# Feed-forward part ordered by a graph of needed-by times, with more seven-product chunks

## Chip, cores and metric

The kernel runs on one core of a Trainium2 chip. The metric is device time in microseconds (us); the median of the runs counts. Engines: PE (TensorE) multiplies matrices and writes PSUM; ACT (ScalarE) and DVE (VectorE) read and write PSUM and SBUF; POOL (GpSimd) works on SBUF alone; SP (SyncE) issues most DMA transfers. Each engine takes its instructions in order.

## Reference

One token block of 2048 rows and width 576 goes through a linear-attention block and through a feed-forward block, and a per-row gate mixes the two.

```python
def _B_ref(x, w1, b1, w2, b2):
    y = _layernorm(x, axis=-1)
    h = _gelu(jnp.einsum("bsd,df->bsf", y, w1) + b1)      # w1: 576 x 4608
    return jnp.einsum("bsf,fd->bsd", h, w2) + b2          # w2: 4608 x 576
x = A_x
g = _sigmoid((x * gate_w).sum(-1, keepdims=True))
a = _A_ref(x, A_wqkv, A_wo)       # linear attention, 32 heads of 18
b = _B_ref(x, B_w1, B_b1, B_w2, B_b2)
return g * a + (1 - g) * b
```

The inputs are float32. Every factor is split into a rounded high part and a low part, so a product is made of high x high, high x low and low x high.

## Kernel before

The attention part comes first (up to about 279 us) and is the same in both kernels, but for the stores named below. Its results, scaled by g, are `acc[0..15]`, sixteen tiles of 128 rows.

The feed-forward part handles the 2048 rows in two halves of 1024 (`NSUP = 2`, `TPS = 8` tiles), and the 4608 hidden columns in 18 chunks of 256 (`NCHUNK`). So there are 36 steps k; `HALF_TIME = 18` begins the second half.

**Up-projection.** Each step computes h for one chunk and 1024 rows as a 2 x 2 block product with seven products in place of eight (Strassen's scheme in Winograd's form, `FACTORS`). One product is seven matmuls of 128 x 512 (`FIVE`), so a step has 49. `A11 ... S4` are the blocks and sums of w1, `B11 ... T4` those of y. Products accumulate in three of four PSUM banks (X, Yb, Z); `kept` copies an intermediate from PSUM to SBUF by ACT, `plus` adds another one by DVE, `gelu` writes the high part and the whole value by ACT and its returned function the low part by DVE.

**Down-projection.** A plain chunk (`down`) makes 8 tiles x 12 matmuls of 128 x 288 = 96, in two alternating PSUM pairs (`ff_pairs`, banks 6-7 and 4-5), and DVE adds each tile, weighted by 1 - g, onto `acc`. A seven-product chunk (`unit`) makes 14 units of 6 matmuls = 84. It needs four sums of w2 blocks (`sum_w2`, POOL, 4 operations) and four sums of h (`sum_h`, POOL, 4 operations), each split by ACT and DVE.

In the first half all 18 chunks are plain. In the second half chunks of steps 18 to 33 (16 of them) are seven-product; each of the seven products has a running sum over all these chunks in `sums` (DVE adds 14 evictions per chunk, ACT writes some of the first), and step 35 puts the seven sums together (`add_sums`, `add_combined`). Steps 34 and 35 (`PLAIN`, `LAST`) are plain.

**Order.** Both loops are written out by hand: the down-projection of step k - 1 runs between the up products of step k, and the jobs for other engines (`later`, `todo`) stand at numbered places. In the first half w1 of the next chunk is loaded, summed (`sum_w1`, POOL), split and stored to DRAM (`w1d`); y of the second half is normalized, summed, split and stored (`load_pair` to `store_pair`). In the second half the split w1 comes back from DRAM, 7 x 320 KB per step, and y is loaded anew at the change of halves. `attend_out` stores the attention tiles of the second half only, to `late_acc`. All instructions pass through one helper, so the profile gives line 109 (`InOrder`) for all; groups are told apart by tile names: `h`, `u` (whole values), `region` (split w2, and other split data), `fresh` (raw w1 and w2), `accs` (sums and accumulators), `wa`, `wb` (split w1), `ps` (PSUM).

Of the kernel before, what the change touches and what calls it, by code (L numbers as in the profile page):

```python
# [43 lines left out]

# [8 lines left out]

FIVE = [(0, 0), (1, 1), (2, 2), (0, 3), (1, 4), (3, 0), (4, 1)]
A11, A12, S2, S1, A21, A22, S3, S4 = range(8)  # L70
FIRST_W, LAST_W = (A11, S1), (A22, S4)
B11, B21, T1, B22, T2, T3, T4 = range(7)

# [4 lines left out]
PLAIN = 2 * NCHUNK - 2  # L78
LAST = 2 * NCHUNK - 1
DOWN_ORDER = (1, 4, 2, 5, 7, 6, 3)  # L80
W2_PLACES = [FACTORS[n][1] for n in DOWN_ORDER]
W2_GROUPS = ((0, 2), (2, 4), (4, 6), (6, 7))
# [30 lines left out]
def tile_gated_mix(ctx: ExitStack, tc: tile.TileContext, x, xm, xe, wm, we, wvm, wve, wo, um, ue, w2, b1, b2, gw, out):  # L113
# [6 lines left out]

# [32 lines left out]
    for _ in range(WARM):  # L153
# [11 lines left out]
    sums = {n: accs[:, i * TPB * HALF:(i + 1) * TPB * HALF].rearrange("p (s n) -> p s n", n=HALF)  # L165
            for i, n in enumerate(DOWN_ORDER)}
# [8 lines left out]
    mrt = keep.tile([2 * max(q1 - q0 for q0, q1 in MOMENTS), P], F32, name="mrt")  # L175
    moments = [dram.tile([2, (q1 - q0) * P], F32, name=f"moments{b}") for b, (q0, q1) in enumerate(MOMENTS)]
    w1d = [dram.tile([P, 7, 5, P], F32, name=f"w1d{c}") for c in range(NCHUNK)]
    late_acc = dram.tile([TPS, P, D], F32, name="late_acc")

# [15 lines left out]

# [119 lines left out]


# [65 lines left out]
    def store_moments(b, p):  # L382
        n = mr[b].shape[1] * mr[b].shape[2]
        act.activation(mrt[:n], p[:n], AF.Copy)
        sp.dma_start(moments[b].rearrange("a (t n) -> (a t) n", n=P), mrt[:n])
# [4 lines left out]

# [30 lines left out]
    def split_pair(sup, j, part, stage):  # L421
        m0, m1 = 2 * part, min(2 * part + 2, 7)
# [316 lines left out]
    for m in (B11, B21, T2, T1, T3, T4, B22):  # L739
        load_y(0, m)  # L740
# [15 lines left out]
    hs, c2s, w2raw = {}, {}, {}  # L756

    def wr(k):
        at_ = fresh[:, :24 * P] if k > 1 else spare[:, :24 * P]
        return at_.rearrange("p (m s n) -> p m s n", m=8, s=3)  # L760
# [9 lines left out]
    def sum_w1(k):  # L770
        r = wr(k)
        for to, x0, x1, op in ((S1, A21, A22, OP.add), (S2, S1, A11, OP.subtract), (S4, A12, S2, OP.subtract),
                               (S3, A11, A21, OP.subtract)):
            pool.tensor_tensor(out=r[:, to], in0=r[:, x0], in1=r[:, x1], op=op)

    def split_w1(k, first):

        a, b = FIRST_W if first else LAST_W
        b += 1
        w = wa if first else wb  # L780
        src = wr(k)[:, a:b]
        act.activation(w[:, :, 0:3], src, AF.Copy)
        dve.tensor_sub(w[:, :, 3:5], src[:, :, 0:2], raw(w[:, :, 0:2]))
        dve.tensor_sub(w[64:P, :, 2], src[64:P, :, 2], raw(w[64:P, :, 2]))
# [4 lines left out]

    def w1_of(a):  # L790
        return wa[:, a] if a <= FIRST_W[1] else wb[:, a - LAST_W[0]]

    def load_split_w1(k, a):
        place = a if a <= FIRST_W[1] else a - LAST_W[0] + 4
        sp.dma_start(raw(w1_of(a)).rearrange("p s n -> p (s n)"),
                     w1d[k % NCHUNK][:, place].rearrange("p s n -> p (s n)"))

    def w2_rows(k):
        c = k % NCHUNK
        return w2[c * CF * P:(c + 1) * CF * P].rearrange("(f p) d -> p f d", p=P)  # L800

    def load_w2(k, to):
        w2raw[k] = to.rearrange("p (f n) -> p f n", f=CF)
        sp.dma_start(w2raw[k], w2_rows(k))

    def split_w2(k, to, parts=(0, 1)):
        c2 = c2s[k] = to.rearrange("p (a f n) -> p a f n", a=2, f=CF)
        if 0 in parts:
            act.activation(c2[:, 0], w2raw[k], AF.Copy)
        if 1 in parts:  # L810
            dve.tensor_sub(c2[:, 1], w2raw[k], raw(c2[:, 0]))

    def product(k, n, p, start=True, part=range(len(FIVE))):
# [5 lines left out]
        if len(FIVE) - 1 in part:  # L819
            if k == HALF_TIME - 1:  # L820
                load_y(1, b)
            if HALF_TIME - 1 <= k < LAST:
                load_split_w1(k + 1, a)
# [7 lines left out]
    def plus(t, p):  # L831
        dve.tensor_tensor(out=t, in0=p, in1=t, op=OP.add)
        return t

    def gelu(k, f, t, src, whole, h=None, split=True):

        bias = b1s[:, k % NCHUNK * CF + f:k % NCHUNK * CF + f + 1]
        if split:
            h = hs[k, f, t] = take_h((k, f, t)) if h is None else h
            act.activation(h[:, 0], src, AF.Gelu_apprx_tanh, bias=bias)  # L840
        act.activation(whole, src, AF.Gelu_apprx_tanh, bias=bias)
        return lambda: dve.tensor_sub(h[:, 1], whole, raw(h[:, 0]))

    TERMS = ((0, 0), (0, 1), (1, 0))
    terms = [(f, a, w) for f in range(CF) for a, w in TERMS]

    def add(i, to, term):
        dve.scalar_tensor_tensor(to, term, omg[:, PLACE[i]:PLACE[i] + 1], to, op0=OP.mult, op1=OP.add)

    def down_terms(p, s, k, half, only=range(len(terms)), opens=True, closes=True):  # L850
        c0 = s % TPB * P
        for n in only:
            f, a, w = terms[n]
            pe.matmul(p, hs[k, f, s // TPB][:, a, c0:c0 + P], c2s[k][:, w, f, half_cols(half)],
                      start=opens and n == 0, stop=closes and n == len(terms) - 1)

    def down(k, s):

        if k >= 0:
            p = two_of(ff_pairs)[:, :, :HALF]  # L860
            for n in range(len(terms)):
                for half in range(2):
                    down_terms(p[:, half], s, k, half, (n,))
            if s % TPB == TPB - 1:
                give_back_h((k, 0, s // TPB), (k, 1, s // TPB))
            add(s, halves(acc[s]), p)
            if k == 1 + s:
                add(s, acc[s], b2b)
            if k == HALF_TIME - 1:
                sp.dma_start(out[s * P:(s + 1) * P, :], acc[s])  # L870
        for job in later.get((k + 1, s), ()):
            job()
# [3 lines left out]
    b2b = ffc.tile([P, D], F32, name="b2b")  # L876
    wa = ffc.tile([P, FIRST_W[1] - FIRST_W[0] + 1, 5, P], F32R, name="wa")
    wb = ffc.tile([P, LAST_W[1] - LAST_W[0] + 1, 5, P], F32R, name="wb")

# [4 lines left out]
    extra[3] += [lambda: sp.dma_start(b2b, everywhere(b2, D))]  # L884
    extra[5] += [lambda: sum_w1(0), lambda: act.activation(tiny, ones[:, 0:1], AF.Gelu_apprx_tanh)]
    extra[7] += [lambda: split_w1(0, True), lambda: store_w1(0, True)]
    extra[9] += [lambda: split_w1(0, False), lambda: load_w1(1), lambda: store_w1(0, False)]
    extra[11] += [lambda: sum_w1(1)]

# [17 lines left out]

    h_places = ctx.enter_context(tc.tile_pool(name="hp", bufs=1)).tile([P, 6, 2, SB], F32R, name="h")
    h_free, h_taken = list(range(6)), {}

    def take_h(key):
        h_taken[key] = h_free.pop(0)
        return h_places[:, h_taken[key]]

    def give_back_h(*keys):
        h_free.extend(h_taken.pop(key) for key in keys)

    up = ctx.enter_context(tc.tile_pool(name="up", bufs=6))


    fresh = ctx.enter_context(tc.tile_pool(name="fresh", bufs=1)).tile([P, 33 * P], F32, name="fresh")
    region = ctx.enter_context(tc.tile_pool(name="region", bufs=1)).tile([P, 56 * P], F32R, name="region")
    y_stage = [region[:, n * 10 * P:(n + 1) * 10 * P].rearrange("p (m s n) -> p m s n", m=2, s=5) for n in range(2)]
    w2_whole = fresh[:, 24 * P:33 * P]
    c2_places = [region[:, (20 + 18 * n) * P:(38 + 18 * n) * P] for n in range(2)]
    w2_sums = fresh[:, :7 * HALF].rearrange("p (m n) -> p m n", n=HALF)
    s_places = [region[:, 14 * HALF + n * 2 * SB:][:, :2 * SB].rearrange("p (a n) -> p a n", a=2)
                for n in range(3)]
    load_w2(0, w2_whole)

    later = {}

    def after(k, s, f, *args):
        later.setdefault((k + s // 8, s % 8), []).append(lambda: f(*args))

    for j in range(4):
        k, s = divmod(15 + 28 * j, TPS)
        after(k, s, load_pair, 1, j)
        for n in range(4):
            after(k, s + 6 + n, normal_pair, 1, j, n // 2, n % 2)  # L940
            after(k, s + 10 + n, sum_pair, 1, j, n)
        for part in range(4):
            after(k, s + 14 + 3 * part, split_pair, 1, j, part, lambda part=part: y_stage[part % 2])
            after(k, s + 15 + 3 * part, split_tails, 1, j, part)
            after(k, s + 16 + 3 * part, store_pair, 1, j, part)

    def load_w2_blocks(k):
        rows_ = w2_rows(k)
        for f, (m0, m1) in enumerate(((B11, B12), (B21, B22))):
# [287 lines left out]
```

## Time and profile before

| | |
|---|---|
| median of 3 runs | 1130.14 us (1129.23 to 1131.17) |
| span of the profiled execution | 1127.9 us; the median of the runs lies 2.2 us above it (its own time is not listed apart) |
| matmuls in the span | 6886 |
| granted PE clock | 1.000 |
| DMA | 189.84 MB, mean 168 GB/s |

How to read the lines: a row of the timeline or of the chain begins with its start and its duration in us; "x7" counts merged instructions; square brackets give the idle time of the engine just before, and what ended it. A group's row ends with total busy us, mean ns of one | idle us before. A matmul's duration includes its way through the array, so the distance from start to start is what counts. The windows give busy us of each engine in a stretch, with the number of instructions.

### The profile page before, as it was taken

How to read it: one execution, taken by the hardware profiler on the slowest of the kernel's cores; microseconds unless marked ns; L12 is line 12 of the kernel's file. 1: busy time of each engine (PE TensorE's matmuls, PEld its weight loads, DVE VectorE, ACT ScalarE, POOL GpSimd, SP SyncE). 2: the span in 40 equal slices, each digit the busy share in tenths (PEclk: the TensorE clock that was granted, in tenths of full speed). 3: DMA queues.
4: the chain of work that ended last, by engine and by line, in shares of the span. 5: the costliest groups of instructions: out<-in, count | busy, mean ns of one | idle time of the engine just before them, and what ended most of it. 6: DMA issues, size and time to landing. Idle time of an engine off the chain costs nothing.

```text
span 1127.9 us, 18132 instructions
## 1 busy us (share of the span) xinstructions
PE 1116.1 (99%) x6886; PEld 1022.6 (91%) x6886; DVE 862.3 (76%) x1292; ACT 555.6 (49%) x950; POOL 308.4 (27%) x252
## 2 busy tenths in 40 slices
PE   9999999999999999999999999999999999999998
PEld 8999989999899999999999999988999899989988
DVE  4567775895669878778778765678899889888985
ACT  6667664443545444545444543455444544454441
POOL 2111112342111123112122111234453445344530
PEclk9999999999999999999999999999999999999999
DMA  6267854524454764555755549744444444444452
GB/s 183 58 112 262 174 165 185 232 93 144 172 168 171 230 220 155 210 168 191 241 190 175 189 165 385 292 134 121 123 136 136 122 121 136 136 120 123 137 174 84
DMA packets 102984, 189.84 MB, mean 168 GB/s; under 512 B 8300, under 2 KB 58748, under 8 KB 98674
## 3 DMA queue, kind: packets, MB, share of 16 engines
q1 hardware_dynamic: 102018, 187.94, 51.7%
q8 instruction: 54, 0.88, 0.3%
q10 hardware_dynamic: 720, 0.74, 0.2%
q14 instruction: 32, 0.26, 0.1%
q0 software_dynamic: 160, 0.01, 0.0%
HBM read 121.93 MB, written 66.73 MB: 167 GB/s over the span
## 4 chain that ended last, share of the span: by engine, by line
PE 87%; DVE 6%; ACT 3%; issue 2%; DMA 1%; SPq 0%; ACTq 0%; DVEq 0%
PE ps L109 87%; DVE den L109 1%; DVE accs L109 1%; DVE qt L109 1%; DVE region L109 1%; DVE acc L109 0%; DVE u L109 0%; DMA t<-in_xe 0%; DMA s<-in_we 0%; DMA s<-in_wm 0%; DVE y L109 0%; ACT L109 0%; ACT h L109 0%; ACT u L109 0%; SPq L109 0%
## 5 line engine op out<-in xcount | busy, mean ns | idle before, releaser
L109 PEld LDWEIGHTS ps<-region,h 128*128 128x128 f32 x2568 | 368.5, 188 | 23.1 <-DVE accs L109 1.0
L109 PE MATMUL ps<-region,h 128*128 128x288 f32 x2568 | 383.1, 295 | 0.9 <-DVE fresh L109 0.7
L109 PE MATMUL ps<-y,wa 128*128 128x512 f32 x1008 | 265.0, 392 | 0.0
L109 POOL TENSOR_TENSOR fresh<-fresh 128x384 f32<-128x384 f32 (+1 forms) x128 | 138.1, 1084 | 438.2 <-DMA fresh<-in_ue 175.0
L109 PE MATMUL ps<-y,wb 128*128 128x512 f32 x756 | 201.1, 395 | 1.0 <-ACT u L109 1.0
L109 PEld LDWEIGHTS ps<-y,wa 128*128 128x128 f32 x1008 | 177.8, 188 | 26.2
L109 DVE TENSOR_TENSOR accs<-ps,accs 128x576 f32<-128x576 f32 x210 | 158.0, 753 | 32.3 <-PE ps L109 22.7
L109 ACT ACTIVATE h<-u,b1s 128x512 fp32r<-128x512 f32 x90 | 65.3, 725 | 215.7 <-DVE u L109 215.7
L109 PEld LDWEIGHTS ps<-y,wb 128*128 128x128 f32 x756 | 132.9, 188 | 23.3 <-ACT u L109 1.7
L109 DVE SCALAR_TENSOR_TENSOR accs<-ps,omg,accs 128x576 f32<-128x576 f32 (+1 forms) x146 | 118.1, 810 | 45.0 <-PE ps L109 44.0
L109 ACT ACTIVATE u<-ps 128x512 f32<-128x512 f32 x108 | 63.8, 591 | 149.3 <-PE ps L109 149.0
L109 POOL TENSOR_TENSOR u<-u 128x512 f32<-128x512 f32 x64 | 100.2, 1566 | 126.0 <-ACT u L109 122.2
L109 PE MATMUL ps<-y 128*128 128x288 f32 (+1 forms) x896 | 126.5, 297 | 3.2 <-DVE acc L109 2.0
L109 PEld LDWEIGHTS ps<-y 128*128 128x128 f32 x896 | 122.2, 188 | 6.6 <-DVE acc L109 2.7
L109 DVE TENSOR_TENSOR h<-u,h 128x512 fp32r<-128x512 f32 x142 | 104.8, 738 | 27.3 <-ACT u L109 27.2
L109 ACT ACTIVATE u<-u,b1s 128x512 f32<-128x512 f32 x108 | 78.3, 725 | 53.9 <-DVE u L109 50.9
L109 DVE TENSOR_TENSOR u<-ps,u 128x512 f32<-128x512 f32 x108 | 74.2, 687 | 36.3 <-ACT u L109 23.3
L109 PEld LDWEIGHTS ps<-region 128*128 128x128 f32 x600 | 90.3, 188 | 8.9 <-ACT accs L109 0.5
L109 DVE TENSOR_TENSOR region<-fresh,region 128x576 fp32r<-128x576 f32 (+1 forms) x83 | 80.9, 975 | 20.7 <-ACT region L109 20.7
L109 PE MATMUL ps<-region 128*128 128x288 f32 x600 | 96.2, 295 | 0.1
L109 PE MATMUL ps<-wp,qt 128*128 128x288 f32 x448 | 63.6, 298 | 0.9 <-DVE qt L109 0.9
L109 PEld LDWEIGHTS ps<-wp,qt 128*128 128x128 f32 x448 | 59.9, 188 | 1.4 <-DVE qt L109 1.4
(136 smaller groups left out, 1056.2 us busy)
## 6 DMA issues: line engine op xcount, KB each, us to landing
w1d<-wa SPq DMA_DIRECT2D x18, 1280.0 KB
wa<-w1d SPq DMA_DIRECT2D x72, 320.0 KB
y<-yd SPq DMA_DIRECT2D x14, 1280.0 KB
w1d<-wb SPq DMA_DIRECT2D x18, 960.0 KB
wb<-w1d SPq DMA_DIRECT2D x54, 320.0 KB
fresh<-in_w SPq DMA_DIRECT2D x20, 576.0 KB
fresh<-in_w SPq DMA_DIRECT2D x32, 288.0 KB
fresh<-in_um SPq DMA_DIRECT2D x64, 128.0 KB
```

Source lines behind the costliest of these rows:

```text
L109: return lambda *args, **kwargs: self.tc.keep_in_program_order(op(*args, **kwargs))
```

## The change

- The hand-written loops go. Every operation of the feed-forward part on PE, ACT, DVE, POOL and of the DMA queue becomes an `Op` with what it needs, what it gives, a duration and a tail. Due times run backward from PE's nominal order; then a list scheduler issues operations engine by engine (`choose`, `commit`). PE has two lines, up products and down units, and takes whichever can begin, the unit first when it comes at most 100 ns after the up product and is due. Operations on two SBUF tensors (`port=True`) are kept apart between DVE and POOL in the plan.
- `SEVEN`: steps 1, 3, ..., 15 and 17 to 34 are seven-product, the other ten plain.
- `chunk_of`: the second half begins with chunk 17, whose w1 and w2 are still there.
- No running sums: M1, M2 and so on accumulate in PSUM. `FORK` copies M1 to the other PSUM pair by ACT; 6 of 7 units per half are evicted, by DVE, onto `acc`. In a plain chunk with k > 0 four of eight units (`SEEDS`) start from a copy of the accumulator in PSUM and are copied back by ACT; the other four are added by DVE. b2 is the start of the first chunk.
- `acc` now holds b alone: all 16 attention tiles go to `late_acc` and come back (`load_attn`); `weighed` mixes them at the end of each half.
- The up order becomes 1, 5, 6, 2, 7, 4, 3; for k > 0 the first intermediate is copied from bank X to bank Yb by ACT, and product 2 accumulates onto it. Split w1 is cut in three groups, stored y in 28 pieces instead of 16; w2 has 7 places, h 9, u 5.

```diff
-DOWN_ORDER = (1, 4, 2, 5, 7, 6, 3)
+SLOTS = 14
+LAG = 3
+SEVEN = {*range(1, NCHUNK - 1, 2), *range(NCHUNK - 1, LAST)}
+UP_ORDER = (1, 5, 6, 2, 7, 4, 3)
+H_BUFS, U_BUFS, W2_BUFS = 9, 5, 7
+EARLY, LATE_, SLOP, SLACK = 0, 3, 30, 300
+SEEDS = ((0, 0, 0), (0, 1, 0), (1, 0, 0), (1, 1, 0))
+DOWN_ORDER = (1, 2, 6, 5, 7, 3, 4)
+OPENS, TAKES = (1, 2, 5), ((2, 6, 5, 4) if FORK else (1, 6, 5, 4))
...
-        if i >= TPS:
-            sp.dma_start(late_acc[i - TPS], acc[i])
+        sp.dma_start(late_acc[i], acc[i])
...
+    def chunk_of(k):
+        return k if k < HALF_TIME else (k + NCHUNK - 1) % NCHUNK
...
+    def make_units(k):
+        if k in SEVEN:
+            todo = [(q, n) for q in range(2) for n in DOWN_ORDER]
+            for j, (q, n) in enumerate(todo):
+                p = next(pair_next)
...
+                if forked:
+                    op(ACT, lambda p=p: copy(pair_ap(p), pair_ap(10 - p)), needs=[("unit", k, 1, q)] + pair_users[p],
+                       gives=[("forked", k, q)], ns=563, tail=650)
+                    needs = needs + [("forked", k, q)]
...
+                op(PE, lambda n=n, q=q, p=p, opens=opens: one_of_seven(k, n, q, p, opens), ns=6 * 132.3,
+                   tail=6 * 132.3 + 165, needs=needs, gives=[unit], by=("down", k, j, len(todo)),
...
+                evict(k, t, q, half, n in TAKES, p, unit, False)
+        else:
+            todo = [(half, q, t) for half in range(2) for q in range(2) for t in range(2)]
...
+                if seeded:
+                    op(ACT, lambda p=p, half=half, q=q, t=t: copy(pair_ap(p), start_of(k, acc_of(t, q, half), half, True)),
...
+    def evict(k, t, q, half, first, p, unit, seeded):
...
+        if seeded:
+            op(ACT, lambda: copy(to, pair_ap(p)), needs=needs, gives=[key], ns=543, tail=653)
         else:
+            op(DVE, lambda: add_to(to, pair_ap(p), start_of(k, to, half, first)), 2 * HALF, needs=needs, gives=[key])
...
+    def make_sum(k, m):
+        to, x0, x1, how = H_SUMS[m]
...
+        op(engine, lambda: eng.tensor_tensor(out=us((k, to)), in0=us((k, x0)), in1=us((k, x1)), op=how), SB,
+           needs=needs, gives=[("sum", k, m)], port=True)
+        op(ACT, lambda: copy(h_of((k, m))[:, 0], us((k, to))), SB, needs=[("sum", k, m)], gives=[("hi", k, m)],
+           take=("h", [(k, m)]))
...
+            if a and b:
+                behind = next_up - b.slot
+                if b.slot > next_up + EARLY:
+                    tb = None
+                if behind > LATE_:
+                    ta = None
+                if ta is not None and tb is not None:
+                    if tb <= ta + 100 and behind >= 0 or tb < ta:
+                        ta = None
+                    else:
+                        tb = None
```

More of the change, by code (lines that the diff above doesn't have):

```diff
@@ L832, in plus, with bias_of, split_all_w1 @@
         dve.tensor_tensor(out=t, in0=p, in1=t, op=OP.add)
[L833 to L872, printed above, removed]
+    def bias_of(k, f):
+        return b1s[:, chunk_of(k) * CF + f:chunk_of(k) * CF + f + 1]
     weigh(3)
     ffc = ctx.enter_context(tc.tile_pool(name="ffc", bufs=1))
-    b2b = ffc.tile([P, D], F32, name="b2b")
     wa = ffc.tile([P, FIRST_W[1] - FIRST_W[0] + 1, 5, P], F32R, name="wa")
     wb = ffc.tile([P, LAST_W[1] - LAST_W[0] + 1, 5, P], F32R, name="wb")
+    def split_all_w1(k, first):
+        a0, a1 = FIRST_W if first else LAST_W
+        for part in range(3):
+            split_w1(k, a0, a1 + 1, part)
     extra = {i: [] for i in range(NT)}
@@ L929, in tile_gated_mix @@
[L929 to L945, printed above, removed]
@@ new lines, in tile_gated_mix @@
+    region = ctx.enter_context(tc.tile_pool(name="region", bufs=1)).tile([P, W2_BUFS, 2, HALF], F32R, name="region")
+    y_stage = ctx.enter_context(tc.tile_pool(name="ystage", bufs=1)).tile([P, 2, 5, P], F32R, name="ystage")
+    acc8 = accs[:, spare.shape[1]:].rearrange("p (s n) -> p s n", n=D)
+    attn = [spare[:, n * D:(n + 1) * D] for n in range(6)] + [fresh[:, n * D:(n + 1) * D] for n in range(2)]
+    PE, ACT, DVE, POOL, DMA = "PE", "ACT", "DVE", "POOL", "DMA"
+    COST = {ACT: (90, 0.838, 97), DVE: (65, 1.0425, 83), POOL: (30, 2.5, -40)}
@@ L1177, in tile_gated_mix @@
[L1177 to L1198 removed]
+                pe.matmul(pair_ap(p)[:, j], h[:, x, c0:c0 + P], w[:, y], start=opens and i == 0,
+                          stop=i == len(TERMS) - 1, skip_group_check=not opens)
@@ new lines, in weighed, with make_finish @@
+    def weighed(sup, s, to, x, y):
+        n = PLACE[sup * TPS + s]
+        dve.scalar_tensor_tensor(to, x, omg[:, n:n + 1], y, op0=OP.mult, op1=OP.add)
+    def make_finish(sup, needs):
+        for s in range(TPS):
+            t, q = s // TPB, s % TPB // 2
+            done = [key for half in range(2) for key in acc_users[t, q, half]]
+            op(DVE, lambda s=s: weighed(sup, s, attn[s], acc[s], attn[s]), D, needs=done + needs(s),
+               gives=[("fin", sup, s)], port=True, more=60)
+            if sup == 0:
+                for half in range(2):
+                    acc_users[t, q, half] = acc_users[t, q, half] + [("fin", sup, s)]
+                dma(lambda s=s: sp.dma_start(out[s * P:(s + 1) * P, :], attn[s]), [("fin", sup, s)], [("out", s)],
+                    450, 2500)
@@ new lines, in commit_free, with room_time, when_ @@
+    def commit_free(o):
+        give_keys(o, o.ready - 0)
+    for o in begin:
+        offer(o)
+    def room_time(o):
+        if not o.take:
+            return 0.0
+        name, keys = o.take
+        if lines[name][0] is not o or len(rooms[name]) < len(keys):
+            return None
+        return sorted(t for t, _ in rooms[name])[len(keys) - 1]
+    def when_(o):
+        r = room_time(o)
+        if r is None:
+            return None
+        s = max(free[o.engine], o.ready, r)
+        if o.port:
+            other = POOL if o.engine == DVE else DVE
+            s = max(s, port_until[other] - 135)
+        return s
@@ L1202 @@
+    while any(pending.values()):
+        picks = [(x[0], n, x[1]) for n, e in enumerate((PE, ACT, DVE, POOL, DMA)) if (x := choose(e))]
+        assert picks, {e: [(o.by, o.gives, o.needs) for o in v][:3] for e, v in pending.items()}
+        s, _, o = min(picks, key=lambda x: x[:2])
+        commit(s, o)
+    assert not any(missing[o] for o in ops), [o.gives for o in ops if missing[o]][:5]
 def kernel(A_x, A_wqkv, A_wo, B_x, B_w1, B_b1, B_w2, B_b2, gate_w):
```

779 lines of the change are left out of this document (501 added, 278 removed).

## The prediction

> **What bounds the kernel now.** I read the page's busy table and clock first, then the chain of waits, then the PE timeline, then windows of ten steps. A step is one chunk's up-projection (49 matmuls of 512 columns) beside the previous chunk's down-projection (96 matmuls of 288 columns when plain, 84 with seven products). A unit is one group of down matmuls that is evicted together.
>
> ```profile
> span 1127.9 us, 18132 instructions
> PE 1116.1 (99%) x6886; PEld 1022.6 (91%) x6886; DVE 862.3 (76%) x1292; ACT 555.6 (49%) x950; POOL 308.4 (27%) x252
> PEclk9999999999999999999999999999999999999999
> ...
> 293.49 445.03 PE ps L109 x2690
> ...
> 755.09 326.92 PE ps L109 x1925
> ```
>
> Two pieces of the chain, 772 of 1128 us, are matmul after matmul with nothing between, and the granted clock is full throughout. PE alone sets the feed-forward part. The pitch shows that busy is not idle in disguise:
>
> ```profile
> 402.01 1.75 PE L109 MATMUL ps<-region,h 128*128 128x288 f32 x12
> 403.59 1.77 PE L109 MATMUL ps<-y,wb 128*128 128x512 f32 x7
> 405.20 1.75 PE L109 MATMUL ps<-region,h 128*128 128x288 f32 x12
> ...
> 836.69 1.09 PE L109 MATMUL ps<-y,wa 128*128 128x512 f32 x4
> 837.62 0.95 PE L109 MATMUL ps<-region,h 128*128 128x288 f32 x6
> 838.41 0.86 PE L109 MATMUL ps<-y,wa 128*128 128x512 f32 x3
> 839.11 0.95 PE L109 MATMUL ps<-region,h 128*128 128x288 f32 x6
> ```
>
> From start to start, 12 matmuls of 288 take 1.58 us (0.132 each) and 7 of 512 take 1.61 us (0.230 each). In the second half a half product takes 0.70 (three matmuls) or 0.93 us (four), a unit of six 0.79.
>
> ```profile
> core 0: us, PE busy (x) PEld busy (x) DVE busy (x) ACT busy (x) POOL busy (x), PEclk, DMA share, GB/s
> 411.58:651.12 239.54, 239.54 (x1452) 218.77 (x1451) 187.52 (x253) 114.83 (x153) 51.02 (x40) 1.00 0.56 192
> 791.55:1017.28 225.73, 225.73 (x1332) 203.52 (x1331) 199.90 (x281) 106.66 (x180) 98.67 (x80) 1.00 0.44 129
> 279.11:291.31 12.20, 11.51 (x52) 9.08 (x51) 4.27 (x6) 7.13 (x10) 0.00 (x0) 1.00 0.38 139
> 291.31:315.76 24.45, 24.29 (x146) 21.83 (x145) 17.78 (x23) 13.11 (x18) 5.02 (x4) 1.00 0.45 152
> 722.99:768.97 45.98, 45.84 (x268) 40.46 (x267) 34.91 (x47) 25.77 (x44) 18.82 (x16) 1.00 0.45 136
> ...
> 699.03:722.99 23.96, 23.96 (x148) 21.87 (x147) 11.29 (x16) 6.46 (x11) 2.55 (x3) 1.00 0.94 375
> 1085.02:1124.31 39.29, 38.07 (x243) 34.78 (x241) 25.92 (x32) 9.56 (x14) 6.38 (x2) 1.00 0.35 123
> ```
>
> The first two rows are ten plain steps (23.95 us each) and ten seven-product steps (22.57). The others are the opening step, the one after it, the first two seven-product steps, the step that changes halves, and the last one to PE's last matmul.
>
> **The change, part by part.** *Fewer matmuls.* Before, chunks 0 to 17, 34 and 35 are plain (20); after, 0, 2, ..., 16 and 35 (10). Ten chunks go from 96 to 84 matmuls: 120 fewer. By matmul pitch that is 120 x 0.132 = 15.8 us. I take the step rows instead, since they carry the finer interleaving too: 10 x (23.95 - 22.57) = **-13.8 us**.
>
> *Stalls that go.* Step 1 costs 24.45 - 23.95 = 0.5 over plain, the first two seven-product steps 45.98 - 45.14 = 0.8, and the last step 39.29 against 49 x 0.230 + 192 x 0.132 = 36.6, so 2.7.
>
> ```profile
> 741.29 1.17 ACT L109 ACTIVATE accs<-ps 128x576 f32<-128x576 f32 x2
> 741.98 1.06 PE L109 MATMUL ps<-region 128*128 128x288 f32 x6
> ...
> 1102.10 2.11 PE L109 MATMUL ps<-y,h 128*128 128x288 f32 x14 [0.20 <-DVE h L109]
> 1104.88 1.86 PE L109 MATMUL ps<-region,h 128*128 128x288 f32 x12 [0.67 <-DVE fresh L109]
> ```
>
> In the middle PE waits for ACT's first evictions into the seven running sums; at the end it waits for DVE, which is putting these sums together. Neither exists afterwards. In step 1 the first unit waits for the split of all of w2 (0.39 <-DVE region, below); afterwards it needs two blocks of four and comes three half products later. At the end, eight weighed adds of attention tiles take the sums' place on DVE, so I count 2.0 of 2.7: **-3.3 us** in all (bounds: 0 and -4.0). The opening step stays: product 4 still follows product 7 into the same bank with nothing between.
>
> *Forks.* Each seven-product chunk now copies M1 from one PSUM pair to the other on ACT before product 2, twice: 52 copies. PSUM to PSUM is not in the trace. The nearest case is that opening stall, a PE to ACT to PE round trip with no cover:
>
> ```profile
> 285.49 1.77 PE L109 MATMUL ps<-y,wb 128*128 128x512 f32 x7
> 287.29 0.60 ACT L109 ACTIVATE u<-ps 128x512 f32<-128x512 f32 x1 [0.52 <-PE ps L109]
> 287.94 3.53 PE L109 MATMUL ps<-y,wb 128*128 128x512 f32 x14 [0.69 <-ACT u L109]
> ...
> 293.49 0.69 PEld L109 LDWEIGHTS ps<-region,h 128*128 128x128 f32 x5 [0.39 <-DVE region L109]
> ...
> L109 ACT ACTIVATE accs<-ps 128x576 f32<-128x576 f32 x8 | 5.1, 648 | 3.5 <-PE ps L109 3.5
> ```
>
> Seven matmuls from 285.49 would hand over at 287.10; the next start is at 287.94: 0.84 us. With 0.65 instead of 0.60 for 576 columns it is 0.89. A half product in between covers 0.70 or 0.93, so 0.20 or nothing shows, and two cover all. The order puts an up half product ahead when the unit would come over 0.1 us late. Bounds 0 and 52 x 0.20 = 10.4; I take 0.05 each, nearer zero because of that rule: **+2.6 us**. If ACT is busy with another copy the wait grows by up to that copy.
>
> *Seeds.* A plain unit whose PSUM starts from a copy of its accumulator (ACT) and is copied back by ACT pays 2 x 0.65 plus hand-overs, about 1.6; between two uses of its pair PE has another unit (1.58) and some 2.8 us of up products. Zero; uncovered, 32 x 1.6 = 51.
>
> *DVE and POOL in the first half.* Two steps (a plain and a seven-product chunk) offer 23.95 + 22.57 = 46.5 us.
>
> ```profile
> L109 DVE TENSOR_TENSOR accs<-ps,accs 128x576 f32<-128x576 f32 x140 | 105.5, 753 | 21.0 <-PE ps L109 15.4
> L109 DVE TENSOR_TENSOR u<-ps,u 128x512 f32<-128x512 f32 x30 | 20.5, 684 | 4.9 <-ACT u L109 4.9
> L109 POOL TENSOR_TENSOR u<-u 128x512 f32<-128x512 f32 x40 | 63.1, 1577 | 70.0 <-ACT u L109 67.7
> L109 POOL TENSOR_TENSOR fresh<-fresh 128x288 f32<-128x288 f32 x40 | 35.6, 890 | 57.0 <-DMA fresh<-in_w 54.6
> ...
> L109 DVE TENSOR_TENSOR h<-u,h 128x512 fp32r<-128x512 f32 x40 | 27.8, 695 | 9.4 <-ACT u L109 9.3
> L109 DVE SCALAR_TENSOR_TENSOR accs<-ps,omg,accs 128x576 f32<-128x576 f32 x81 | 65.9, 813 | 16.3 <-PE ps L109 15.7
> ```
>
> DVE starts from 187.52 / 5 = 37.5 us per two steps. Evictions stay 16 but cost 0.753 instead of 0.813 (-1.0); adds of product pairs fall from 6 to 4 (-1.4); low parts of h rise from 8 to 11 (+2.1); three more w2 blocks and the finer cutting of w1 and y cost, estimated from these rows, +2.6. Sum 39.8, or 86%. POOL goes from 51.02 / 5 = 10.2 to 10.2 + 4 x 1.577 + 4 x 0.890 = 20.1. The second half of before ran DVE at 199.90 / 225.73 = 89% with POOL at 44% and no stall, so I cost this at zero; the lock below is what speaks against it. In the second half DVE sheds 2 evictions and an add per step (2.2 us).
>
> *Latency of the sums of h* (S1, S3, S2 in a row, then split): 3 x 1.58 + 0.6 + 0.7 = 6 us after H21, and S2 is due about seven half products and seven units later, 11 us. Zero, with 4 us to spare; what comes later than that, PE waits for.
>
> *Order of chunks and transfers.* The second half opens with the weights already there, so seven 320 KB loads go. They cost nothing before: that step took 23.96 us at DMA share 0.94. Eight more 288 KB attention tiles are stored and read back, 1.5 us each at the 192 GB/s of the first half, under steps that use 0.56 of DMA. On SP the first two stores stand ahead of the first chunk's w1 load and wait for ACT's scaling of their tiles; that load is used four tiles later. Zero; uncovered, about 3 us once.
>
> **Sum:** -13.8 - 3.3 + 2.6 = -14.5. The profiled span becomes 1127.9 - 14.5 = 1113.4; the median lies 2.2 us above the span, so 1130.1 - 14.5 = **1115.6 us**.
>
> **Rivals.** *Slower: the lock between DVE and POOL stretches the first half.*
>
> ```profile
> 838.22 6.54 POOL L109 TENSOR_TENSOR u<-u 128x512 f32<-128x512 f32 x4 [6.83 <-ACT u L109]
> 841.83 0.75 DVE L109 TENSOR_TENSOR accs<-ps,accs 128x576 f32<-128x576 f32 x1
> 842.50 1.12 DVE L109 TENSOR_TENSOR region<-u,region 128x512 fp32r<-128x512 f32 x1
> ...
> 847.42 0.68 DVE L109 TENSOR_TENSOR region<-u,region 128x512 fp32r<-128x512 f32 x1
> ```
>
> Beside POOL, a DVE operation that reads two SBUF tensors takes 1.12 instead of 0.68, one that reads PSUM its usual 0.75. End to end, DVE and POOL would need 39.8 + 20.1 = 59.9 us per two steps, so 13.4 of POOL's 20.1 (67%) must hide behind DVE's PSUM reads and idle time. The second half of before hid at least 19.99 + 9.87 - 22.57 = 7.3 of 9.87 (74%). The two-SBUF work is 39.8 - 16 x 0.753 - 4 x 0.684 = 25.0; with POOL's 20.1 it makes 45.1 of 46.5, and an eviction queued behind a locked DVE operation holds PE. It turns slower from 14.5 / 8 = 1.8 us per pair of steps, under 58% hidden. With half hidden: 8 x (49.9 - 46.5) = +27, **1142.6 us**. Chance 0.14.
>
> The Trainium skill ("SBUF — State Buffer", "SBUF: two separate sides") calls this an exclusive lock for a whole instruction between GpSimd and a VectorE operation with two SBUF inputs. The two 1.12/0.68 rows agree; by it the 25.0 and 20.1 above cannot overlap at all, which leaves the sum as it is but only 1.4 us of room.
>
> *Forks show in full:* each waits 0.20 because ACT (busier by forks and seeds) serves it a half product late: 10.4 instead of 2.6, **1123.4 us**. For it: ACT is in-order and copies take 0.6 to 0.73. Against: PE can place another half product. Chance 0.20.
>
> *The change doesn't do what it says:* the matmuls go, but PE waits as long for h or w2 blocks in the seven-product steps of the first half, 8 x 1.38 = 11.0 us, and new edges bring stalls like the 3.3 that go: 1115.6 + 14.3 = **1129.9 us**. Against it is the 4 us of slack. Chance 0.04.
>
> **Numbers.** Forecast 0.62 (with all stalls gone and no fork waits, -13.8 - 4.0, it ends at 1112.3; a little under that if the finer interleaving costs less). Its own range is 1110.5 to 1119. The range 1110.5 to 1124.5 takes in the forks and leaves out the lock and what lies below. A difference under 0.2% (2.3 us) can't be told from no change: faster 0.82, same 0.04, slower 0.14.
>
> **What would show it.** PE has 6766 matmuls. First-half steps alternate between about 23.95 and 22.6. The opening step keeps its 0.84; the last one, from its first up product to the last matmul, falls to 49 x 0.230 + 180 x 0.132 = 35.0 and little more. DVE is near 86% and POOL near 43% in the first half. Gaps in PE released by ACT after the first unit of each seven would be the forks; gaps released by DVE with POOL at 1.6 us per add would be the lock. Steps of two over 48 us in the first half make the prediction wrong.

## The result, and the profile after

| | median (lowest to highest), us | ratio to before, 95% interval |
|---|---|---|
| before, six runs | 1130.68 (1129.23 to 1131.89) | |
| after, six runs | 1126.07 (1123.76 to 1128.62) | 0.9961 (0.9951 to 0.9971) |

The change makes the kernel faster by 0.39%. That is 4.6 us, a third of the 14.5 us forecast, and the time lies above the range.

The head of the page after, the 40 slices of PE's clock, and the chain's shares:

```profile
span 1124.1 us, 18584 instructions
PE 1108.0 (99%) x6766; PEld 1003.5 (89%) x6766; DVE 888.7 (79%) x1369; ACT 642.6 (57%) x1153; POOL 385.9 (34%) x325
PEclk9999999999999999999999999999999999999999
...
PE 72%; DVE 14%; ACT 4%; DMA 4%; issue 3%; POOL 2%; SPq 1%; ACTq 0%; DVEq 0%; POOLq 0%
```

The 120 matmuls went, as counted: 6886 to 6766. At 0.132 us each that is 15.8 us of PE's work, but the span fell by only 1127.9 - 1124.1 = 3.8. PE still reads 99% busy, because a matmul's record ends late and covers short gaps. So the loss has to be looked for stage by stage. The next table takes each stage from the first up-projection matmul of its first step to that of the step after its last one (for the last stage, to the end of PE's last matmul), in the profiled executions.

| stage, us | before | after | expected by the prediction's terms |
|---|---|---|---|
| start of step 0 | 279.11 | 279.60 | no change |
| steps 0 and 1 | 36.65 | 34.68 | -0.5 |
| steps 2 to 17 | 383.27 | 381.28 | 8 x -1.38 = -11.0, forks +0.8 |
| steps 18 and 19 | 47.03 | 46.84 | -1.38 - 0.5, forks +0.2 |
| steps 20 to 33 | 316.37 | 317.93 | -0.3, forks +1.4 |
| steps 34 and 35 | 61.88 | 60.50 | -1.38 - 2.0, forks +0.2 |

Steps 0-1 and 34-35 belong together: with `LAG = 3` some units of a chunk run after the next step has begun, so work leaves the early step and comes back in the last one: 12 matmuls fewer begin in steps 0 and 1 (194 to 182), and 374 in steps 34 and 35 as before. Together they gave 3.35 us of the 3.7 expected. Of the 10.7 us that are missing (14.5 - 3.8), 8.2 are missing in steps 2 to 17 and 1.5 in steps 18 and 19. (The 0.8 that the prediction names for the first two seven-product steps lies in steps 19 and 20, 0.5 and 0.3.) The windows of steps 2 to 17, before and then after, give busy us and instructions of each engine, the clock and DMA:

```profile
315.76:699.03 383.27, 383.27 (x2322) 350.05 (x2321) 293.54 (x392) 181.53 (x241) 77.12 (x62) 1.00 0.59 203
```

```profile
314.27:695.55 381.28, 376.98 (x2226) 334.90 (x2225) 331.36 (x475) 243.93 (x401) 157.12 (x124) 1.00 0.55 191
```

96 matmuls are gone (2322 to 2226), 12.7 us, and the stage is 2.0 us shorter. DVE is at 331.36 / 381.28 = 87% and POOL at 41%: the loads that I foresaw (86% and 43%). The steps don't alternate between 23.95 and 22.6, as they should; they lie anywhere from 22.8 to 24.5.

How much of that is waiting? I took every distance from matmul start to matmul start in this stage that exceeds its pitch (0.132 or 0.230 us) by more than 0.03 us. The excess adds up to 0.0 us before and **11.2 us** after. The view of waits of the same stage says who ended PE's idle time (total us, times, longest; PEld is PE's weight load, ahead of the matmul):

```profile
ACT h L109 <- POOL u L109: 8.1, 7, 1.6
PEld ps L109 <- ACT ps L109: 6.8, 14, 1.1
PEld ps L109 <- DVE accs L109: 5.1, 7, 1.1
...
PE ps L109 <- DVE accs L109: 2.0, 5, 0.7
...
PEld ps L109 <- DVE wa L109: 1.7, 5, 0.8
...
PE ps L109 <- ACT ps L109: 1.4, 3, 0.7
```

PE waits for ACT's copies inside PSUM (`ps <- ps` and `ps <- accs`: the forks, the copies of the first intermediate, and the seeds) and for DVE's evictions into `accs`. The first row matters as much: ACT's own copies of the h sums wait 8.1 us for POOL. Two places in the timeline after show how this hangs together. First an eviction behind locked work:

```profile
428.10 4.01 POOL L109 TENSOR_TENSOR fresh<-fresh 128x384 f32<-128x384 f32 x3
...
428.50 1.77 DVE L109 TENSOR_TENSOR accs<-accs 128x768 f32<-128x768 f32 x1
...
430.19 1.41 DVE L109 TENSOR_TENSOR accs<-ps,accs 128x576 f32<-128x576 f32 x2
...
430.99 1.06 PE L109 MATMUL ps<-region,h 128*128 128x288 f32 x6 [0.66 <-DVE accs L109]
```

POOL adds pieces of the next w1 for 4 us. A DVE operation on SBUF data alone starts in the same stretch and takes 1.77 us, where its group's mean in this stage is 1.01; the eviction queued behind it comes late, and PE stands for 0.66 us. Then a fork behind the copies of sums:

```profile
411.08 3.52 POOL L109 TENSOR_TENSOR u<-u 128x512 f32<-128x512 f32 x2
...
412.86 1.15 ACT L109 ACTIVATE h<-u 128x512 fp32r<-128x512 f32 x2 [1.18 <-POOL u L109]
...
413.92 0.67 ACT L109 ACTIVATE region<-fresh 128x576 fp32r<-128x576 f32 x1
414.12 2.45 DVE L109 TENSOR_TENSOR h<-u,h 128x512 fp32r<-128x512 f32 x2
414.50 0.62 ACT L109 ACTIVATE h<-u 128x512 fp32r<-128x512 f32 x1
...
415.02 0.63 ACT L109 ACTIVATE ps<-ps 128x576 f32<-128x576 f32 x1
...
415.70 1.85 PE L109 MATMUL ps<-region,h 128*128 128x288 f32 x12
```

POOL's two sums take 3.52 us. ACT, which takes its instructions in order, waits 1.18 us for the first of them, and only after that, a split and another copy does it reach the fork at 415.02. PE's unit starts when the fork is done. Beside POOL, two low parts of h take DVE 2.45 us; before, one took 0.695. The groups of the stage after (mean ns of one behind the busy us) say the same in the mean:

```profile
L109 DVE TENSOR_TENSOR h<-u,h 128x512 fp32r<-128x512 f32 x88 | 77.2, 892 | 6.0 <-ACT u L109 4.3 <-ACT h L109 1.5
...
L109 POOL TENSOR_TENSOR u<-u 128x512 f32<-128x512 f32 x32 | 50.8, 1586 | 7.2 <-DVE h L109 3.5 <-ACT u L109 2.5
```

### The profile page after: what moved, and what is told of

It is laid out like the page before. It is cut to its first block, busy times and chain, and to the rows that moved or that the text cites. A ratio compares the mean times of both kernels' runs of the same rounds, so it can differ in the third digit from the quotient of the medians.

```text
span 1124.1 us, 18584 instructions
## 1 busy us (share of the span) xinstructions
PE 1108.0 (99%) x6766; PEld 1003.5 (89%) x6766; DVE 888.7 (79%) x1369; ACT 642.6 (57%) x1153; POOL 385.9 (34%) x325
## 4 chain that ended last, share of the span: by engine, by line
PE 72%; DVE 14%; ACT 4%; DMA 4%; issue 3%; POOL 2%; SPq 1%; ACTq 0%; DVEq 0%; POOLq 0%
PE ps L109 72%; DVE accs L109 3%; DVE h L109 3%; DMA fresh<-in_w 2%; DVE region L109 2%; SPq L109 1%; DVE wa L109 1%; POOL u L109 1%; DVE wb L109 1%; DVE den L109 1%; ACT h L109 1%; ACT u L109 1%; POOL fresh L109 1%; DVE u L109 1%; DMA w1d<-wb 0%
## 5 line engine op out<-in xcount | busy, mean ns | idle before, releaser
L109 PEld LDWEIGHTS ps<-region,h 128*128 128x128 f32 x3144 | 453.7, 188 | 45.9 <-DVE accs L109 10.0
L109 PE MATMUL ps<-region,h 128*128 128x288 f32 x3144 | 480.9, 296 | 4.0 <-DVE accs L109 2.0
L109 DVE TENSOR_TENSOR accs<-ps,accs 128x576 f32<-128x576 f32 x336 | 250.3, 752 | 89.8 <-PE ps L109 87.0
L109 POOL TENSOR_TENSOR fresh<-fresh 128x288 f32<-128x288 f32 (+1 forms) x164 | 173.8, 1066 | 406.2 <-DMA fresh<-in_w 332.0
L109 DVE TENSOR_TENSOR h<-u,h 128x512 fp32r<-128x512 f32 x222 | 177.1, 811 | 7.2 <-ACT u L109 4.3
L109 POOL TENSOR_TENSOR u<-u 128x512 f32<-128x512 f32 x104 | 152.3, 1465 | 88.1 <-DVE h L109 46.8
L109 DVE TENSOR_TENSOR region<-fresh,region 128x576 fp32r<-128x576 f32 x120 | 107.8, 898 | 2.4 <-ACT region L109 1.9
L109 ACT ACTIVATE region<-fresh 128x576 fp32r<-128x576 f32 x120 | 73.9, 628 | 33.9 <-PE ps L109 33.9
L109 ACT ACTIVATE h<-u 128x512 fp32r<-128x512 f32 x104 | 60.2, 622 | 12.4 <-POOL u L109 12.2
L109 DVE TENSOR_TENSOR wa<-fresh,wa 128x512 fp32r<-128x512 f32 x64 | 50.6, 791 | 14.8 <-ACT wa L109 13.9
```

What stands on the lines that cost most here:

```text
L109: return lambda *args, **kwargs: self.tc.keep_in_program_order(op(*args, **kwargs))
```

## The experiments

Three causes were set against each other. **The lock** (L): POOL's adds stretch DVE's operations on two SBUF tensors, and evictions come late. **The queue** (Q): the lock, or a slow POOL, makes sums late, and ACT, in order, passes that on to forks, seeds and splits. **The forks themselves** (F): ACT's extra copies. A fourth (R) came up on the way: an edit that makes the scheduler write another order lets the waits fall anew. Theory G of the first expectations is its forerunner: the waits belong to the new order itself.

All stage times below are those of the table above, from each kernel's profiled execution. Repeated runs of after lie up to 4.9 us apart, so a few us in a single profile are not read as an effect; ratios come from several runs beside before on the same chip.

**First half all plain, forks on.**

```diff
-SEVEN = {*range(1, NCHUNK - 1, 2), *range(NCHUNK - 1, LAST)}
+SEVEN = {*range(NCHUNK - 1, LAST)}
```

> All eight seven-product chunks of the first half but chunk 17 made plain again, everything else as after the change. Matmuls rise by 8 x 12 = 96, 12.7 us at 0.132. Theory L (the lock: the first half's 11.2 us of waits in steps 2 to 17 come from DVE operations held up by POOL's sums, which the seven-product chunks add): the waits fall below 1.5 us, steps 2 to 17 take 16 x 23.95 = 383 us, and the span becomes 1124.1 + 12.7 - 10 = 1127. Theory F (forks: the waits come from ACT's copies from pair to pair) says the same, because the forks go as well. Theory G (the waits belong to the new order itself, whatever the products): most of the waits stay, steps 2 to 17 take about 392 us, span about 1136.

Measured 1126.96 us, ratio 0.9971 (0.9960 to 0.9983). The eight seven-product chunks of steps 1 to 15 bring nothing that can be told: 12.7 us of matmuls were put back and the span is 1123.8 us against 1124.1. Steps 2 to 17 take 384.80, with 3.9 us of waits, most of it in two steps of 25.6 and 26.0 us. A plain step under the new order takes 23.80 where nothing waits (before 23.95). G had said a span of 1136 and is out; L and F had both said 1127, so this run doesn't tell them apart. It ties most of the waits to the seven-product chunks.

**The first half's POOL sums without two SBUF inputs.** A sum becomes an 8-column sum and three fills. The rest of each sum is left out, so the products are of other numbers; only the time of this kernel is of use.

```diff
+    def touch(to, x, y, how):
+        pool.tensor_tensor(out=to[:, :8], in0=x[:, :8], in1=y[:, :8], op=how)
+        for _ in range(3):
+            pool.memset(to[:, 8:], 0.01)
...
```

> Same order of instructions, but in the first half (w1 of chunks 2 to 17, w2 and h of chunks 1 to 15) each sum of two tensors on POOL adds only 8 columns and then fills the rest with three memsets, which take about as long as the sum (0.92 ns per column and memset) and read nothing; the sums are left out, so the products are of other numbers. Theory L: with POOL no longer reading SBUF beside DVE, DVE's two-input operations go back to 0.68 us for 512 columns (mean now 0.89 to 1.05 in the first half), and the waits of steps 2 to 17 fall from 11.2 to under 3 us, span about 1115 to 1117. Theory F (ACT's copies are late because ACT is full): ACT's work is unchanged, the waits released by ACT (4.5 us) stay, span above 1119. Theory G (order): waits stay within 2 us, span about 1123.

Measured 1127.80 us, ratio 0.9984 (0.9973 to 0.9994): not faster than after, against the lock theory. The lock was all but gone, the low parts of h taking 0.69 us in the mean, yet the waits rose from 11.2 to 15.3 us. The three fills are slow themselves: with the short sum they take 3 x 0.519 + 0.322 = 1.88 us for 512 columns, against 1.59 for the add in after, so POOL ran later. The groups, the view of waits and a piece of the timeline of this kernel:

```profile
L109 POOL MEMSET u<- 128x504 f32 x90 | 46.7, 519 | 3.5
...
L109 POOL TENSOR_TENSOR u<-u 128x8 f32<-128x8 f32 x30 | 9.7, 322 | 2.6 <-DVE h L109 2.1 <-ACT u L109 0.5
```

```profile
ACT h L109 <- POOL u L109: 19.3, 8, 4.1
PEld ps L109 <- ACT ps L109: 14.1, 12, 3.3
...
PE ps L109 <- ACT ps L109: 9.5, 6, 2.8
```

```profile
509.93 1.68 POOL L109 MEMSET u<- 128x504 f32 x3
...
511.64 1.15 ACT L109 ACTIVATE h<-u 128x512 fp32r<-128x512 f32 x2 [3.68 <-POOL u L109]
...
512.69 0.67 ACT L109 ACTIVATE region<-fresh 128x576 fp32r<-128x576 f32 x1
...
513.27 0.61 ACT L109 ACTIVATE h<-u 128x512 fp32r<-128x512 f32 x1
...
513.79 0.63 ACT L109 ACTIVATE ps<-ps 128x576 f32<-128x576 f32 x1
...
514.47 2.49 PE L109 MATMUL ps<-region,h 128*128 128x288 f32 x12 [2.83 <-ACT ps L109]
```

ACT waits 3.68 us for POOL, the fork stands behind it in the queue, and PE waits 2.83 us for the fork. (The idle times of PEld and PE overlap. By starts of matmuls, 11.0 of the 15.3 us stand directly behind ACT's copies in PSUM, and 1.7 are matmuls at a granted clock of 0.50 after the wait of 2.83 us.) This is theory Q in the open, with no lock in play: a POOL that is late holds PE by way of ACT.

**Forks off.** M1 is then evicted by DVE once more per half chunk.

```diff
-FORK = True
+FORK = False
```

> Forks off: M1 is evicted by DVE like the others, 14 evictions per seven-product chunk instead of 12 and two copies on ACT. Theory F: the 4.5 us of first-half waits released by ACT go, span about 1120. Theory L: DVE gets 52 more evictions (0.67 us each, 35 us over the run), its first half goes from 87% to 90% busy, and waits released by DVE evictions take the place of those by ACT; span 1123 to 1128. In the second half, where no wait is seen beyond 0.3 us per step, both expect 22.57 to 22.7 us per step.

Measured **1120.71 us**, ratio 0.9917 (0.9900 to 0.9935), clearly below after. That is what F had said (about 1120), and not what L had said (1123 to 1128). Steps 2 to 17 take 377.99. Steps 20 to 33 take 316.03 in place of 317.93, which is (317.93 - 316.03) / 28 = 0.07 us for each of the 28 forks there; the kernel with a plain first half has the same forks and takes 316.54, 0.02 each, which is even less than without them (316.81, the kernel with both edits below). The 0.05 of the prediction lies in that range. In steps 2 to 17 DVE is busier than in after (338.89 us, third engine column), and PE still waits less:

```profile
313.94:691.93 377.99, 376.18 (x2227) 335.35 (x2226) 338.89 (x492) 235.63 (x385) 157.25 (x124) 1.00 0.56 193
```

**Two fills in place of three.** As the second experiment but `range(2)`, so that POOL is no later than an add would be alone: two fills and the short sum make 2 x 0.520 + 0.343 = 1.38 us for 512 columns, where an add takes 1.59 in after and 1.29 in the three cases of the kernel with a plain first half. The sums are left out here too.

> As in e2_no_lock (first half: each sum of two tensors on POOL adds 8 columns and fills the rest with memsets that read nothing; the sums are left out), but with two memsets instead of three: 0.20 + 2 x 0.52 = 1.24 us for 512 columns, where three took 1.76 and a real sum takes 1.29 alone and 1.69 beside DVE. Same order, forks on. Theory Q (the lock makes POOL and DVE late; ACT, in order, waits for POOL's sums with copies that stand ahead of the copies PE needs): with POOL on time and no lock, the waits of steps 2 to 17 fall from 11.2 to under 3 us, those steps take about 373 to 375 us and the span is about 1116. If lateness of POOL was not the cause (theory F, ACT simply full), the 4.5 us released by ACT's PSUM copies stay and the steps take over 377 us.

Measured **1116.82 us**, ratio 0.9877 (0.9860 to 0.9893): 9.3 us below after, with all forks and seeds in place. Its windows, waits and groups in steps 2 to 17:

```profile
313.90:686.01 372.11, 371.89 (x2226) 336.82 (x2225) 290.03 (x475) 244.32 (x401) 132.95 (x357) 1.00 0.56 196
```

```profile
PEld ps L109 <- ACT ps L109: 1.1, 4, 0.3
```

```profile
L109 DVE TENSOR_TENSOR h<-u,h 128x512 fp32r<-128x512 f32 x88 | 59.5, 691 | 6.2 <-ACT u L109 5.3 <-ACT h L109 0.8
...
L109 POOL MEMSET u<- 128x504 f32 x58 | 30.2, 520 | 1.7
...
L109 POOL TENSOR_TENSOR u<-u 128x8 f32<-128x8 f32 x29 | 9.9, 343 | 11.4 <-ACT u L109 6.9 <-DVE h L109 4.5
```

2.0 us of waits are left, most steps alternate between 22.56 and 23.85, and no copy of ACT waits for POOL's sums any more. The order of the instructions on PE, DVE, ACT and POOL is that of after, fills apart, here and with three fills, so R can't be the reason. ACT carries the same 401 instructions as in after and the same 244 us, so its load was never the trouble. Both of the earlier suspects have their answer: the lock is the cause, and without it, but with a late POOL, the waits come back (second experiment). What PE feels is lateness, of DVE and POOL, carried by in-order queues. Which side of the lock weighs more isn't separated: it stretches DVE's operations and POOL's adds at once, and two fills take away both.

**Every third chunk, forks off,** to give the sums more time: `{*range(1, NCHUNK - 2, 3), *range(NCHUNK - 1, LAST)}`.

> Forks off and seven products in every third step of the first half (1, 4, 7, 10, 13) and from 17 on: 3 x 12 = 36 matmuls more than e3_no_fork, 4.75 us. Theory Q: two plain steps in a row give POOL and DVE room, so a seven-product chunk costs less than the 7.8 / 8 = 1 us of waits that it costs in e3_no_fork; the first half's waits fall to about 2 to 3 us and steps 2 to 17 take about 377 to 379 us, equal to 378.0 of e3_no_fork. If the waits belong to each seven-product chunk alone, 5 us remain and the steps take 381.

Measured 1134.87 us, ratio 1.0040 (1.0026 to 1.0053): slower than before, a miss. The reason is another queue. In the timeline ACT stands for 7.44 us before a copy into `ystage` whose place a store still holds, with a seed behind it:

```profile
451.07 0.52 ACT L109 ACTIVATE ystage<-accs 128x384 fp32r<-128x384 f32 x1 [7.44 <-DMA yd<-ystage]
...
453.50 0.64 ACT L109 ACTIVATE ps<-accs 128x576 f32<-128x576 f32 x1
...
454.20 3.25 PE L109 MATMUL ps<-region,h 128*128 128x288 f32 x12 [4.85 <-ACT ps L109]
```

This run says nothing on the spacing of the chunks, since two such waits of about 5 us, each with matmuls at half clock behind it, drown it.

**Forks off, first half plain** (both edits).

> Forks off and no seven-product chunk in the first half but chunk 17: 96 matmuls (12.7 us) more than e3_no_fork. Theory Q: almost no waits are left in steps 2 to 17, which take 16 x 23.80 = 380.8 us plus under 1 us; the span is about 1117.5 + 3 = 1120.5. So with the forks off the eight seven-product chunks of the first half give back 3 of 12.7 us. Against e1_plain_first (the same with forks, 1123.8): if forks cost nothing where no sums compete on POOL, the difference stays under 1 us outside the two long steps of e1_plain_first.

Measured 1126.76 us, ratio 0.9962 (0.9947 to 0.9976), about the same as with forks on (0.9971); I had expected a larger gain (a span of 1120.5; it is 1123.9). Two long steps (25.4 and 25.9) stand in the first half again. So the forks cost nothing that can be told where no sums of h compete for ACT's queue, and 1126.07 - 1120.71 = 5.4 us where they do. Seen the other way, with forks off the eight chunks do pay: the span falls from 1123.9 to 1117.5.

**Less of the lock.** In plain chunks two of four low parts of h are formed from PSUM, with forks on, then with forks off (`SLACK` 100), and beside them the kernel without forks with another order alone (`SLACK` 600).

```diff
+        in_ps = k not in SEVEN and not whole_taken
+        whole = src if in_ps else lambda: us((k, which))
...
+            op(DVE, lambda: minus(h_of((k, which))[:, 1], whole(), raw(h_of((k, which))[:, 0])), SB,
```

> After the change, but in plain chunks the whole values of two of four h blocks are written by ACT into their PSUM bank, so that DVE forms the low part from PSUM and SBUF and needs no lock: 2 x 0.68 us of locked work per plain chunk fewer, about 1.4 of some 41 us per pair of steps. Theory Q: first-half waits fall from 11.2 to 7 to 9 us, time about 1122 to 1124. Rival R (the waits are single copies standing behind late ones on ACT, and any new order draws them anew, as in e5_every_third): the waits change by several us either way, unrelated to the locked work; 1118 to 1135.

> The same with forks off (and the scheduler's SLACK at 100 ns instead of 300). Theory Q: first-half waits fall from the 7.8 us of e3_no_fork to 5 to 6, time about 1118 to 1119.5, the fastest of the right kernels. Rival R: 1116 to 1130.

> e3_no_fork with SLACK at 600 ns instead of 300: the same work and the same locked work, another order. Theory Q alone: within 2 us of e3_no_fork (1120.7). Rival R: away from it by more than 2 us, with the difference in one or two long waits that ACT releases.

Measured 1123.48 us (ratio 0.9943, 0.9927 to 0.9959), 1123.46 us (0.9937, 0.9923 to 0.9952) and 1121.41 us (0.9911, 0.9890 to 0.9931). With forks on the waits of steps 2 to 17 fall from 11.2 to 8.4 us, as Q says, though steps 18 and 19 give 4 us back in the profiled run. With forks off and another slack the same edit doesn't help (12.8 us of waits against 7.8), which misses Q's 1118 to 1119.5 and lies in R's range. The slack alone moves the waits to 9.8 in one profile, but the time by only 0.7 us, within the 2 us that Q had named. So R is neither shown nor out: the order may account for a few us, and the edit is not separated from that. The two kernels without forks whose sums are otherwise as in after (0.9917 and 0.9911, not told apart) are the fastest of those that keep every sum whole, and the intervals of both lie wholly below that of after.

The kernels that argue for the cause, side by side (us, profiled executions; waits as defined above):

| | after | plain, forks | forks off | two fills | plain, forks off |
|---|---|---|---|---|---|
| steps 2 to 17 | 381.28 | 384.80 | 377.99 | 372.11 | 384.85 |
| of it PE's waits | 11.2 | 3.9 | 7.8 | 2.0 | 4.0 |
| DVE, low part of h, mean | 0.892 | 0.699 | 0.844 | 0.691 | 0.700 |
| steps 18 to 33 | 364.77 | 361.75 | 361.69 | 365.07 | 361.93 |
| span | 1124.1 | 1123.8 | 1117.5 | 1114.6 | 1123.9 |

## Why the prediction was right in sign and wrong in size

- **Fewer matmuls, -13.8: right.** 6766 as named. Where nothing waits, steps alternate by 1.29 us, near the 1.38 that I took: 23.85 to 22.56 in the kernel with two fills.
- **Stalls that go, -3.3: right where it was large.** The ends gave 3.35 of 3.7 together with their chunk. The last step by itself takes 37.5 us and not 35.0, since 241 matmuls fall into it in place of the 49 + 180 = 229 counted (`LAG`): 12 x 0.132 = 1.6 us more, and 0.9 of waits. In the middle step 20 lost its stall (22.91 to 22.69), but step 19 grew from 23.08 to 24.12, with a stall of the new kind, 1.10 us:

```profile
722.94 1.67 ACT L109 ACTIVATE h<-u 128x512 fp32r<-128x512 f32 x3 [3.04 <-POOL u L109]
...
724.52 0.57 ACT L109 ACTIVATE ps<-ps 128x512 f32<-128x512 f32 x1
...
725.15 1.19 PE L109 MATMUL ps<-y,wa 128*128 128x512 f32 x4 [1.10 <-ACT ps L109]
```

- **The opening step stays: right, but the stall grew.** It still stands after product 7, and by starts it is 288.71 - 285.97 - 1.61 = 1.13 us in place of 0.84:

```profile
285.97 1.75 PE L109 MATMUL ps<-y,wb 128*128 128x512 f32 x7
...
288.71 0.50 PE L109 MATMUL ps<-y,wb 128*128 128x512 f32 x1 [1.00 <-ACT u L109]
```

- **Forks, +2.6 for 52: right by themselves** (0.07 each or less in the second half), with the condition I wrote beside it, that the wait grows if ACT is busy with another copy, and then left out of the sum. In the first half ACT stood waiting for POOL, so a fork's wait was not bounded by a copy's length. The rival that forks show in full (1123.4) is near the measured time, but its reason, a busier ACT, is refuted by the kernel with two fills; that closeness is luck.
- **DVE and POOL in the first half, cost at zero: this is the step that failed.** The loads came out as named (87% and 41%), but DVE's partly by luck: its 39.8 us for two steps was a sum without the lock, and the same instructions without it take 290.03 / 8 = 36.3; with it they take 331.36 / 8 = 41.4. The sign that I had named showed as well: steps 6 and 7 take 48.7 us together, over 48. I judged the loads by throughput: 67% of POOL's time had to hide, the second half had hidden 74%. But it is not enough that the work fits. The lock stretches single operations (in this stage a low part of h takes up to 1.78 us in place of 0.68, a POOL add up to 1.82 in place of 1.29), and what comes late stands in an in-order queue in front of something PE needs. Why the second half of before bore the same loads is open: its evictions went into sums that nobody read until the end, and its sums of h had no fork behind them, but neither reason was run. The second half of after speaks against the forks as the whole reason. It has them behind its sums of h too, POOL is 41% busy, and ten steps there run at 22.70 us each with hardly a wait; DVE, however, is at 177.24 / 226.96 = 78% and not 87%. The price in the first half is 9.3 us by medians, 11.2 - 2.0 = 9.2 by PE's waits.

```profile
787.99:1014.95 226.96, 226.96 (x1333) 202.68 (x1331) 177.24 (x251) 120.03 (x200) 92.34 (x80) 1.00 0.46 128
```

- **Latency of the sums of h, 4 us to spare: too narrow a question.** No wait of PE in steps 2 to 17 is put down to h itself. But ACT's copies waited for POOL seven times in the stage, up to 1.6 us, and what was late was the copies' successors on ACT, which that count left out.
- **The lock as the slower rival (1142.6): the mechanism was right,** evictions behind locked operations included, and mis-sized. Its 27 us came from half of POOL's time being unhidden. In fact it never made DVE the bound; it made single results late by 0.5 to 1.1 us. I gave it one all-or-nothing price where a partial one belonged in the likeliest case.
- **The rest of the sum is borne out as a total:** with the first half's lock taken out the time is 1116.82 against the 1115.6 forecast. Part of this is luck, since errors cancel: steps 2 to 17 come out 1.0 us better than forecast there (372.11 against 383.27 - 10.2), and steps 18 to 33, which keep POOL's adds, 2.3 us worse (365.07 against 363.40 - 0.6). So the zeros for seeds, loads and stores are not each confirmed.

The Trainium skill ("SBUF — State Buffer", "SBUF: two separate sides") says that a DVE operation with two SBUF inputs and a GpSimd operation that reads SBUF take their shared port pair for a whole instruction, and the one that comes second is blocked. The runs agree in so far as both sides get longer: 0.69 us for a low part with fills beside it, 0.89 in the mean and 1.2 each in the stretch shown with adds beside it.

What stays open: why the two kernels with a plain first half have two long steps each (before the wait of 1.37 us in one of them ACT had stood 3.37 us for POOL's sums of w1; it wasn't separated), why the second half of before bore its loads, which side of the lock weighs more, and how much is to be won by fixing the order in which DVE and POOL take the lock, which wasn't tried.

## What to carry to other kernels

On engines that take instructions in order, ask of each busy pair not only whether the work fits into the time but what stands behind each operation when its rival makes it late. A copy that PE needs should not queue behind one that waits for the slowest engine. When an engine's work is to be tested as a cause, make the replacement no slower than the original: three fills hid the answer that two fills gave. Matmuls saved are worth only what the slowest helper lets through: here the eight chunks of the first half were worth nothing with forks (the span is 0.3 us shorter without them) and 6.4 us with the forks off.

## What the runs showed of the hardware

Fills on POOL didn't disturb DVE's operations on two SBUF tensors: with 58 fills of 504 columns in the stage, the low parts stayed at 691 ns, where adds on POOL made them 892.

In the kernel with every third chunk, the wait of 4.85 us was followed by matmuls at half speed. The windows behind it, with the granted clock as the third number from the end:

```profile
454.20:457.20 3.00, 3.00 (x12) 3.00 (x13) 2.96 (x7) 2.19 (x4) 0.00 (x0) 0.50 0.46 191
457.20:460.20 3.00, 3.00 (x9) 2.35 (x8) 3.00 (x5) 2.42 (x4) 0.00 (x0) 0.50 0.96 341
```

Twelve matmuls of 288 columns take the whole of the first 3 us, 0.25 each in place of 0.132, at a clock of 0.50. A long wait thus cost PE more than its length. Shorter waits were followed by the same clock: in the kernel with three fills the one of 2.83 us (0.50 from 515.41 us on, for 3.41 us), and in the kernel with forks and two low parts formed from PSUM one of 1.47 us with another of 0.40 shortly behind it (0.50 from 726.39 on, for 3.41 us). A wait of 2.08 us in the kernel with three fills, and those of up to 1.10 us in after, left it at 1.00, so the length alone doesn't decide. The Trainium skill ("TensorE: Matmul & The Clock Gate", "Part 1: The HAM clock gate") has it that the clock halves after an idle window of about 3.4 us. The wait of 4.85 us agrees; those of 2.83 and 1.47 us are shorter than that window, so here the measurement decides.
